# Row maxima beside the projections, all taken as key differences: 208 double steps a layer, 20 pairs a block in attention

## The chip, the cores and the metric

The kernel runs on one core of a Trainium2 chip. The core has five engines with their own instruction streams: TensorE (PE in the profile; its weight loads have the row PEld), VectorE (DVE), ScalarE (ACT), GpSimd (POOL), and SyncE (SP), which here issues nearly all DMAs. Each engine executes its instructions in order and waits on semaphores. Matmuls write to PSUM, which has eight banks of 128 x 512 fp32. The metric is the device time of one execution in microseconds (us).

## The reference

Two layers with the same weights, each an attention and a feed-forward part with a residual, on 2048 tokens of width 640 with 32 heads of 20:

```python
def _A_ref(x, wqkv, wo):
    qkv = (x @ wqkv).reshape(B, S, 3, H, Dh).transpose(2, 0, 3, 1, 4)
    q, k, v = qkv[0], qkv[1], qkv[2]
    scores = jnp.einsum("bhqd,bhkd->bhqk", q, k) * (Dh ** -0.5)
    p = _softmax(scores, axis=-1)
    o = jnp.einsum("bhqk,bhkd->bhqd", p, v)
    return o.transpose(0, 2, 1, 3).reshape(B, S, D) @ wo

def _B_ref(x, w1, b1, w2, b2):
    h = x @ w1 + b1
    r = jnp.where(h > 0, h, 0)
    return (r * r) @ w2 + b2

x = A_x
x = x + _A_ref(_layernorm(x), A_wqkv, A_wo)
x = x + _B_ref(_layernorm(x), B_w1, B_b1, B_w2, B_b2)
x = x + _A_ref(_layernorm(x), A_wqkv, A_wo)
x = x + _B_ref(_layernorm(x), B_w1, B_b1, B_w2, B_b2)
```

The sizes are B = 1, S = 2048, D = 640, H = 32, Dh = 20, F = 1536, all in fp32.

## The kernel before

Each layer runs in four stages: projections (`qkv`), attention, output projection, feed-forward. Factors of the projections are split into a high and a low part of a rounded format, so a product is three matmuls (high by high, and the two mixed ones).

**Maxima ahead of scores.** The softmax subtracts the exact row maximum. It has to be known before the scores are made, since it enters the score matmul as two more rows of the query tile (L753 multiplies 62 rows, 60 of the three split products and 2 of the maximum). So the product of queries and keys is made twice. First it is made with queries on the partitions (`by_queries`, L659), and VectorE reduces each 128 x 512 result along the keys. Later it is made with keys on the partitions for the exponentials (`score`, L753). Heads are handled in groups of four. A *block* t is one group and 512 queries: 8 groups by 4 query tiles are 32 blocks. For one block and one tile c of 512 keys there are eight *pairs*: a pair is two matmuls (L659) of 128 queries for two heads. They lie in rows 0 to 59 and 64 to 123 and run side by side on the two row halves of TensorE. Counted in these pairs, each layer has 32 blocks x 4 key tiles x 8 = 1024 pairs.

**Single and double steps.** A single step is a pair, with a `tensor_reduce` on VectorE for each of its two results. A double step finds the maximum over two key tiles k1 and k2 from max(q·k1, q·k2) = relu(q·(k1 − k2)) + q·k2. `step_two` makes a pair with the key difference `kd`, and ScalarE writes its relu to SBUF (L692). `both_two` makes a pair with the other key tile, and VectorE adds and reduces in one custom operation for each result, followed by a read of its accumulator (L699). So a double step takes two pairs on TensorE, but only two operations on VectorE for two key tiles. The difference "d" is of key tiles 0 and 1, "e" of 2 and 3. Differences are made in `proj_end` while keys leave the projection. They are stored to the DRAM tensor `d_kd` and loaded again by `load_kd`, rearranged by heads with six DMAs. Keys (`load_k`) and queries (`load_q`) make the same trip through `d_qk`, with six DMAs each.

**The projections.** There are 40 units of query and key columns (128 columns by 512 tokens, 15 matmuls), the list `UNITS`: first the columns 0 to 3 of token block 0, then the same of block 1, 2 and 3, then the other six columns for all blocks. So units 0 to 3 belong to token block 0, units 4 to 7 to block 1, 8 to 11 to block 2, and 12 to 15 to block 3. The column at place 0 is the first key tile of 128 rows, at place 2 the second, at place 4 the third. Then come 16 V units of 30 shorter matmuls. From unit 4 on each matmul is cut into an upper and a lower half of 64 rows, which run side by side (L356 and L368). The lower halves trail by 19 matmuls (`LAG`), so that after the last V unit 18 lower halves are left alone. After each matmul `between(cost)` pays the cost (1, or 0.65 in a V unit) into a pace; when it is used up, `some()` issues one pair, and the pace rises by `PLAIN_PACE` for a single or `DOUBLE_PACE` for a double. `STEPS` says after which unit which tiles are loaded and which maxima may begin. The same loop advances the normalising of the next token block (`front`): statistics and scaling on VectorE, transposes on TensorE. In layer 1 the rows of token block 2 are transposed in unit 6 and those of block 3 in unit 9; in layer 2 those of block 3 in unit 6.

**Attention.** What is left of the pairs is taken there, before the block that needs it. The order of TensorE is a string of letters, `ORDER_OF_BLOCK`, 16 key tiles of 128 long and repeated. "a" and "b" are a score matmul on one row half with a 128 x 512 exponential behind it (L763). "S" is both at once with one 128 x 1024 exponential. "m" and "n" are a maximum matmul on one row half (L659, reduced at L670). "V" is the value product of one key tile (L768): four heads on four column quarters, which the trace shows as eight matmuls. A *gap* is what lies between two V. `todo` lists what the projections left.

**Queues.** A DMA on SP waits for the data it stores or for the store whose data it loads, and everything behind it in the queue waits too.

## Time and profile before

| what | us |
|---|---|
| median of three runs (3578.84 to 3579.93) | 3579.07 |
| the profiled execution | 3581.79 |
| its span in the trace | 3580.0 |
| TensorE busy | 3555.0 |
| ScalarE busy | 2694.4 |
| VectorE busy | 2643.6 |
| GpSimd busy | 835.1 |

By the value matmuls and the first projections, layer 1 has its projections until about 344.6 us and its attention until about 1388. Output projection and feed-forward follow until about 1801, the projections of layer 2 until 2116, and its second attention until about 3162. In a timeline a row gives the start, the length, the engine, the line of the code, the operation and the tiles, how many were merged, and in brackets the idle time before it with what ended it. In a table by stretches a row gives the stretch, its length, for each engine the busy time and the count of instructions, then the granted clock of TensorE, the busy share of the DMA engines and GB/s. Where the table was asked for one line of the code, only that line's instructions are counted.

### The profile page before, as it was taken

The numbers are of one execution on the slowest core, as the hardware profiler recorded it, in microseconds if no ns is written. First come the engines' busy times: TensorE is split into PE (matmuls) and PEld (weight loads), VectorE is DVE, ScalarE is ACT, GpSimd is POOL, SyncE is SP. The second block draws the span as 40 slices with busy tenths as digits, with TensorE's granted clock in tenths as the row PEclk, the third lists the DMA queues.
The fourth block names the chain that finished last, engine by engine and source line by source line (L and its number), as shares of the span: only waits on it lengthen the run. The fifth ranks groups of instructions, "written<-read, shape, count | busy, mean of one in ns | idle before, by whom it ended". The sixth has DMA issues, their size and how long they took to land.

```text
span 3580.0 us, 70922 instructions
## 1 busy us (share of the span) xinstructions
PE 3555.0 (99%) x25544; PEld 2148.8 (60%) x25544; DVE 2643.6 (74%) x5072; ACT 2694.4 (75%) x4742; POOL 835.1 (23%) x945
## 2 busy tenths in 40 slices
PE   9999999999999999999999999999999999999999
PEld 7898333333333336988989973333333333378998
DVE  8999888888888881445579988888888888625443
ACT  3888999999999995122248889999999999932221
POOL 5440334312121211112143201212121212101110
PEclk9999999999999999999999999999999999999999
DMA  7666454422222136622356652222222121365221
GB/s 242 225 229 195 134 173 144 148 74 73 56 55 57 54 106 203 250 74 74 103 192 226 196 172 67 79 75 61 69 82 57 45 57 51 112 237 206 75 81 37
DMA packets 282799, 433.85 MB, mean 121 GB/s; under 512 B 71188, under 2 KB 130324, under 8 KB 282448
## 3 DMA queue, kind: packets, MB, share of 16 engines
q1 hardware_dynamic: 281920, 427.61, 38.3%
q8 instruction: 203, 3.33, 0.4%
q10 hardware_dynamic: 528, 1.70, 0.2%
q14 instruction: 148, 1.21, 0.1%
HBM read 284.48 MB, written 144.68 MB: 120 GB/s over the span
## 4 chain that ended last, share of the span: by engine, by line
PE 94%; DMA 2%; DVE 2%; ACT 1%; issue 0%; SPq 0%; POOL 0%; ACTq 0%; DVEq 0%; POOLq 0%
PE banks L768 28%; PE banks L336 21%; PE banks L753 18%; PE banks L659 17%; PE banks L368 5%; PE banks L356 5%; PE banks L351 1%; PE banks L466 0%; DMA d_qk<-ev 0%; SPq L76 0%; ACT e L763 0%; DMA few<-d_s 0%; DVE r L1283 0%; DVE h L257 0%; ACT r L1282 0%
## 5 line engine op out<-in xcount | busy, mean ns | idle before, releaser
L763 ACT ACTIVATE e<-banks 128x512 f32<-128x512 f32 (+1 forms) x3460 | 2040.1, 688 | 49.1 <-PE banks L753 10.7
L670 DVE TENSOR_REDUCE mx<-banks 128x1 f32<-128x512 f32 x2560 | 1620.0, 684 | 323.1 <-PE banks L659 276.3
L768 PE MATMUL banks<-e,vg 128*32 128x512 f32 x8192 | 1096.4, 605 | 6.1 <-ACT e L763 5.4
L659 PE MATMUL banks<-k,q 60*128 60x512 f32 x3392 | 1073.1, 411 | 5.0 <-DVE mx L684 3.1
L753 PE MATMUL banks<-q,k 62*128 62x512 f32 x4096 | 1043.3, 440 | 0.0
L753 PEld LDWEIGHTS banks<-q,k 62*128 62x128 f32 x4096 | 513.6, 184 | 741.6 <-ACT e L763 468.0
L659 PEld LDWEIGHTS banks<-k,q 60*128 60x128 f32 x3392 | 573.8, 185 | 205.9 <-ACT e L763 65.6
L699 DVE CUSTOM_DVE_ANT_0 rl<-banks,rl 128x512 f32<-128x512 f32 x704 | 456.7, 688 | 32.6 <-PE banks L659 9.3
L692 ACT ACTIVATE rl<-banks 128x512 f32<-128x512 f32 x704 | 382.2, 601 | 55.5 <-PE banks L659 44.6
L768 PEld LDWEIGHTS banks<-e,vg 128*32 128x32 f32 x8192 | 163.8, 108 | 362.7 <-issue 263.1
L336 PE MATMUL banks<-w,h 128*128 128x320 f32 x2304 | 348.9, 310 | 2.7 <-DVE h L257 2.5
L1282 ACT ACTIVATE r<-banks,b_t 128x512 f32<-128x512 f32 x96 | 66.1, 689 | 375.9 <-PE banks L336 203.0
L336 PEld LDWEIGHTS banks<-w,h 128*128 128x128 f32 x2304 | 339.2, 188 | 11.4 <-DVE h L257 6.4
L336 PE MATMUL banks<-xnT,w 128*128 128x512 f32 x1440 | 329.7, 389 | 0.0
L356 PE MATMUL banks<-xnT,wqk 64*128 64x512 f32 x1080 | 327.9, 395 | 0.0
L368 PE MATMUL banks<-xnT,wqk 64*128 64x512 f32 x1080 | 327.8, 393 | 0.0
L336 PEld LDWEIGHTS banks<-xnT,w 128*128 128x128 f32 x1440 | 269.6, 188 | 55.3
L812 POOL TENSOR_TENSOR few<-few,minus_t 128x16 f32<-128x16 f32 x62 | 179.8, 2900 | 228.4 <-DMA few<-d_s 228.3
L368 PEld LDWEIGHTS banks<-xnT,wqk 64*128 64x128 f32 x1080 | 201.9, 187 | 9.4
L659 PE MATMUL banks<-kd,q 60*128 60x512 f32 x704 | 205.2, 397 | 1.8 <-ACT rl L692 1.0
L356 PEld LDWEIGHTS banks<-xnT,wqk 64*128 64x128 f32 x1080 | 199.7, 187 | 11.1 <-issue 1.9
L268 POOL CAST mr<-nt 128x32 fp32r<-128x32 f32 x64 | 13.4, 210 | 817.8 <-DVE nt L725 817.8
(90 smaller groups left out, 2766.3 us busy)
## 6 DMA issues: line engine op xcount, KB each, us to landing
q<-d_qk SPq DMA_DIRECT2D x888, 80.0 KB
d_qk<-ev SPq DMA_DIRECT2D x80, 512.0 KB
k<-d_qk SPq DMA_DIRECT2D x456, 80.0 KB
x<-d_x SPq DMA_DIRECT2D x96, 320.0 KB
d_o<-ot SPq DMA_DIRECT2D x248, 80.0 KB
ot<-d_o SPq DMA_DIRECT2D x38, 512.0 KB
d_v<-v SPq DMA_DIRECT2D x32, 512.0 KB
vg<-d_v SPq DMA_DIRECT2D x32, 512.0 KB
```

The costliest lines, as they stand in the source:

```text
L336: nc.tensor.matmul(dst, a, b, start=(n == 0), stop=(n == last))
L356: top = nc.tensor.matmul(dst, a[:64], b[:64], start=start, stop=last)
L368: low = nc.tensor.matmul(dst, a, b, start=False, stop=last, skip_group_check=True)
L659: nc.tensor.matmul(dst, q_t[t][b : b + 60, p, sub * P : (sub + 1) * P], k_t[t // NQB, c][b : b + 60, p, :], start=True, stop=True,)
L670: nc.vector.tensor_reduce(maxima(t)[:, 2 * p + par, sub, c : c + 1], dst, axis=AX.X, op=ALU.max)
L692: nc.scalar.activation(r, dst, AF.Relu)
L699: nc.vector.tensor_tensor_reduce(out=r[par], in0=dst, in1=r[par], scale=1.0, scalar=LEAST, op0=ALU.add, op1=ALU.max, accum_out=maxima(t)[: ...
L753: nc.tensor.matmul(dst, k_t[t // NQB, kt // 4][b : b + 62, p, (kt % 4) * P : (kt % 4 + 1) * P], q_t[t][b : b + 62, p, :], start=True, stop ...
L763: nc.scalar.activation(dst, src, AF.Exp, scale=SCALE)
L768: nc.tensor.matmul(acc[32 * h : 32 * h + 32, :], v_t[t // NQB, kt // 8][:, kt % 8, 32 * h : 32 * h + 32], es[p][:, par, :], start=(kt == 0 ...
L812: nc.gpsimd.tensor_tensor(few, few, minus_t, op=ALU.pow)
L1282: nc.scalar.activation(r, dst, AF.Relu, bias=b1_t[:, f : f + 1])
```

## The change

- In attention `ORDER_OF_BLOCK` has 20 "m" and "n" pairs in 16 key tiles where it had 21 (42 letters become 40), and 9 "S" where it had 10. Once no maxima are left, another string, `LAST_ORDER`, with "S" and "V" alone, takes over.
- In the projections the four groups of single steps (32 pairs) are gone. `DOUBLE` has 26 groups of eight double steps where it had 22: 208 steps, or 416 pairs, where 32 single and 176 double steps made 384. Attention is left with 608 pairs in place of 640 a layer.
- `DOUBLE_PACE` is 1.90 where it was 1.97. Maxima begin after unit 8 (double) where singles began after unit 4 and doubles after unit 12.
- Key differences are made for three key row tiles instead of two (`jj < 3`; `d_kd` grows to match). For token block 1 and the first two of them the three steps run on VectorE instead of GpSimd, and the store is issued 6 matmuls after the unit's end where it was 16.

What this does to the order of instructions is shown at three places. In TensorE's queue in the first attention, at the start of the same block of both programs (L753 becomes L756, L659 becomes L662, L768 becomes L771; a value product is two rows of two here). Before:

```order
L753 MATMUL banks<-q_7511,k_1184 128x512 x2
L659 MATMUL banks<-k_4452,q_7568 128x512 x2
L753 MATMUL banks<-q_7511,k_1184 128x512 x2
L659 MATMUL banks<-k_4452,q_7568 128x512
L768 MATMUL banks<-e_5398,vg_7877 32x512 x2
L768 MATMUL banks<-e_5397,vg_7877 32x512 x2
L659 MATMUL banks<-k_4452,q_7568 128x512
L753 MATMUL banks<-q_7511,k_1184 128x512 x2
L659 MATMUL banks<-k_4452,q_7568 128x512 x2
L753 MATMUL banks<-q_7511,k_1184 128x512 x2
```

and of the change:

```order
L756 MATMUL banks<-q_7690,k_1116 128x512 x3
L662 MATMUL banks<-k_4581,q_7856 128x512 x2
L756 MATMUL banks<-q_7690,k_1116 128x512
L771 MATMUL banks<-e_5599,vg_8052 32x512 x2
L771 MATMUL banks<-e_5598,vg_8052 32x512 x2
L756 MATMUL banks<-q_7690,k_1116 128x512 x3
L662 MATMUL banks<-k_4581,q_7856 128x512 x2
L756 MATMUL banks<-q_7690,k_1116 128x512
```

The gaps here hold four scores and two maximum matmuls where they held four and three. Over the 16 gaps of a block ten held seven matmuls and six held six; now it is eight and eight.

SP's queue in the first layer, from the store of unit 3's result on (`ev`; `d_qk<-ev_575` and `d_qk<-ev_529` are unit 4's). Before:

```order
L76 DMA d_qk<-ev_420 128x2x512
L76 DMA x_469<-in_A_x_dram 128x640
L76 DMA x_471<-in_A_x_dram 128x640
L76 DMA x_473<-in_A_x_dram 128x640
L76 DMA x_475<-in_A_x_dram 128x640
L76 DMA k_477<-d_qk 20x2x512 x6
L76 DMA q_484<-d_qk 20x2x512 x6
L76 DMA d_wqk<-wqk_283 128x1024
L76 DMA d_qk<-ev_575 128x2x512
L76 DMA d_kd<-kd_580 128x2x512
L76 DMA k_721<-d_qk 20x2x512 x6
L76 DMA q_728<-d_qk 20x2x512 x6
```

and of the change:

```order
L76 DMA d_qk<-ev_406 128x2x512
L76 DMA x_455<-in_A_x_dram 128x640
L76 DMA x_457<-in_A_x_dram 128x640
L76 DMA x_459<-in_A_x_dram 128x640
L76 DMA x_461<-in_A_x_dram 128x640
L76 DMA d_wqk<-wqk_283 128x1024
L76 DMA d_qk<-ev_529 128x2x512
L76 DMA d_kd<-kd_534 128x2x512
L76 DMA kd_581<-d_kd 20x2x512 x6
L76 DMA k_588<-d_qk 20x2x512 x6
L76 DMA q_595<-d_qk 20x2x512 x6
```

The key and query loads for single steps are gone from ahead of the first key difference. Its store is followed at once by its own load, and the first keys and queries stand behind that load. In layer 2 the same pieces stand in the same order, with nothing between the stores of units 0 to 3 and unit 4's store. TensorE's first maximum matmul, which needs `kd` and `q` of these, stands three matmul steps into unit 9.

TensorE's queue at the end of the projections, from the last of the 18 lower halves (L368) on. Before:

```order
L368 MATMUL banks<-wv_3059,xnT_866 128x320
L368 MATMUL banks<-wv_3162,xnT_866 128x320
L368 MATMUL banks<-wv_3059,xnT_866 128x320
L753 MATMUL banks<-q_2225,k_4443 128x512 x7
L659 MATMUL banks<-k_4846,q_4855 128x512 x2
```

and of the change:

```order
L368 MATMUL banks<-wv_3193,xnT_808 128x320
L662 MATMUL banks<-kd_5013,q_4803 128x512 x2
L662 MATMUL banks<-k_5020,q_4803 128x512 x2
L662 MATMUL banks<-kd_5013,q_4803 128x512 x2
L662 MATMUL banks<-k_5020,q_4803 128x512 x2
L662 MATMUL banks<-kd_5013,q_4803 128x512 x2
L662 MATMUL banks<-k_5020,q_4803 128x512 x4
L756 MATMUL banks<-q_2171,k_4581 128x512 x6
```

Seven pairs now stand between the last projection matmul and the first scores. Beside the units, the program of the change has eight pairs in nearly every unit from 10 to 39 and ten or eleven in a V unit; before, it had two to five in units 5 to 14, seven or eight after that, and nine or ten in a V unit.

The diff, cut to its core:

```diff
@@ proj_end
-        if which and pos < FIRST:
-            if tb % 2 == 0 and jj == 0:
+        if which and jj < 3:
+            if tb % 2 == 0 and jj != 1:
                 keys["of"] = slot([P, 2, QB], F32, "kf")
-            kf = keys["of"][:, jj, :]
+            kf = keys["of"][:, jj % 2, :]
             r = xtile("r")[:, :QB] if tb % 2 else kf
-            split_on_pool(ev[:, 0, :], ev[:, 1, :], dst, r, nc.scalar.copy)
+            split_on_pool(
+                ev[:, 0, :], ev[:, 1, :], dst, r, nc.scalar.copy if pos < FIRST else None
+            )
             if tb % 2:
                 kd = slot([P, 2, QB], F32R, "kd")
-                nc.gpsimd.tensor_sub(kf, r, kf)
-                pool_hi(kd[:, 0, :], kf)
-                pool_lo(kd[:, 1, :], kf, kd[:, 0, :].bitcast(F32))
+                eng = nc.vector if pos < FIRST and tb == 1 else nc.gpsimd
+                eng.tensor_sub(kf, r, kf)
+                eng.tensor_copy(kd[:, 0, :], kf)
+                eng.tensor_sub(kd[:, 1, :], kf, kd[:, 0, :].bitcast(F32))
@@ the tables
     DOUBLE = [
-        [],
-        [(0, 1, "d"), (1, 1, "d"), (2, 0, "d"), (2, 1, "d")],
+        [(0, 0, "d"), (0, 1, "d")],
+        [(1, 0, "d"), (1, 1, "d"), (2, 0, "d"), (2, 1, "d")],
         [(0, 2, "d"), (1, 2, "d"), (2, 2, "d")],
...
+        [(3, 0, "d"), (3, 0, "e")],
     ]
-    PLAIN_PACE = 4.2
-    DOUBLE_PACE = 1.97
+    DOUBLE_PACE = 1.90
     STEPS = {
-        2: [("tiles", (0, 0, 0))],
-        4: [("plain", (0, 0, 0)), ("tiles", (1, 0, 0))],
-        5: [("plain", (1, 0, 0))],
-        7: [("tiles", (0, 0, 1))],
-        9: [("plain", (0, 0, 1)), ("tiles", (1, 0, 1))],
-        10: [("tiles", (0, 1, "d"))],
-        11: [("plain", (1, 0, 1))],
+        6: [("tiles", (0, 0, "d"))],
+        8: [("double", 0)],
+        9: [("tiles", (1, 0, "d"))],
         12: [("double", 1)],
         15: [("double", 2)],
         19: [("double", 3)],
+        26: [("double", 4)],
     }
@@ qkv
-                later(store, 10 if n < FIRST else 16)
+                later(store, 10 if n < FIRST else 6 if tb == 1 and pos in (0, 2) else 16)
@@ attention
     ORDER_OF_BLOCK = (
-        "bbannaVbamnabmVnabmnabVSnanbmVnambabmVSbmnaVSnabmVSnSmVbmamnSVbmanbanVan"
-        "abmbmVbambannVbmabanmVSmbanVSnabmVSnSmVm"
+        "SnabmVSanmbVSanmbVSSmnVnabbanmVnabanmbVbabmnnaVnaabmbmVbmmbanaVnambmbaVb"
+        "amnmbaVnanbabmVSmnabVSmnabVSnabmVSanmbV"
     )
+    LAST_ORDER = "SSSVSSVSSVSV"
...
-            for o in ORDER_OF_BLOCK:
+            for o in LAST_ORDER if min(sm_n) == len(todo) else ORDER_OF_BLOCK:
                 op(o)
```

Left out are the function `one` for single steps, which goes, and the loads of the first keys and queries of attention, which follow the new list of what is left.

More of the change, by code (lines that the diff above doesn't have):

```diff
@@ L882, in qkv @@
     def qkv(first, x_src, rest):
-        pending, groups, work = [], [], []
+        pending = []
         double, twos, begun = [], [], []
@@ L940, in end_group @@
             t = g * NQB + qb
-            rest = [w[0] for w in work[:1] + twos[:1]] + [w[0][0] for w in begun[:1]] + groups + double
+            rest = [w[0] for w in twos[:1]] + [w[0][0] for w in begun[:1]] + double
             if t == 0:
@@ L967, in following @@
             return queue.pop(0)
-        def one():
-            w = following(groups, work)
-            if w:
-                (g, qb, c), p, sub = w
-                smax_two(g * NQB + qb, p, sub, c)
-                done.add((g * NQB + qb, p, sub, c))
-                if (p, sub) == PAIRS[-1]:
-                    end_group(w[0])
         def some():
@@ L992, in some @@
                 return DOUBLE_PACE
-            if groups or work:
-                one()
-                return PLAIN_PACE
             w = following(double, twos)
```

19 lines of the change are left out of this document (9 added, 10 removed).

## The prediction, made before the result was known

> **What bounds the kernel now.** I read the page first, then attention as TensorE issues it, then the projections by stretches, then the start of each.
>
> ```profile
> PE 3555.0 (99%) x25544; PEld 2148.8 (60%) x25544; DVE 2643.6 (74%) x5072; ACT 2694.4 (75%) x4742; POOL 835.1 (23%) x945
> 2643.00:2970.10 327.10, 170.30 (x1280) 25.01 (x1272) 1.00 0.22 60
> 2643.00:2970.10 327.10, 137.22 (x420) 72.00 (x420) 1.00 0.22 60
> 2643.00:2970.10 327.10, 318.91 (x540) 1.00 0.22 60
> 1358.49:1388.32 29.83, 27.43 (x185) 7.55 (x185) 0.00 (x0) 28.71 (x52) 6.08 (x4) 1.00 0.56 171
> ```
>
> TensorE is busy nearly always, but its matmuls overlap, so that alone settles nothing. Rows two to four are one stretch of the second attention, by line: L768 (values), L659 (maxima), L763 (exponentials on ScalarE). 1280 value matmuls are 160 key tiles, ten blocks of 16: 32.71 us a block with 42 maximum matmuls (21 pairs). ScalarE is busy 318.91 of 327.10 us, 97.5%, so it looks like the bound. The last row denies it: the last 16 key tiles of the first attention, with all their exponentials and no maxima, took 29.83 us. ScalarE can therefore do a block in 29.83; the other 2.9 come with the maxima. How, a piece of the timeline shows:
>
> ```profile
> 871.49 0.50 PE L659 MATMUL banks<-k,q 60*128 60x512 f32 x1
> 871.49 0.73 PE L753 MATMUL banks<-q,k 62*128 62x512 f32 x2
> 871.83 0.62 PE L659 MATMUL banks<-k,q 60*128 60x512 f32 x2
> 872.07 0.62 PE L753 MATMUL banks<-q,k 62*128 62x512 f32 x2
> 872.61 1.07 PE L768 MATMUL banks<-e,vg 128*32 128x512 f32 x8
> ...
> 876.85 1.06 PE L768 MATMUL banks<-e,vg 128*32 128x512 f32 x8
> ...
> 879.74 0.73 PE L753 MATMUL banks<-q,k 62*128 62x512 f32 x3
> 880.08 0.39 PE L659 MATMUL banks<-k,q 60*128 60x512 f32 x1
> 880.31 0.39 PE L753 MATMUL banks<-q,k 62*128 62x512 f32 x1
> 880.31 0.40 PE L659 MATMUL banks<-k,q 60*128 60x512 f32 x1
> ...
> 882.54 1.06 PE L768 MATMUL banks<-e,vg 128*32 128x512 f32 x8
> ```
>
> The first four rows fill one gap between value groups: 4 scores and 3 maxima. From 872.61 to 876.85 lie two more such gaps, 2.12 us each. From 876.85 to 882.54 lie three with 4 scores and 2 maxima, as in the second group of rows: 1.90 each. The two kinds run on the two row halves side by side, so 3+4 matmuls take four turns and 3+3 take three; a turn is 0.225 us. Half a turn is wasted in each gap of seven. TensorE's order is the bound of attention.
>
> In the projections:
>
> ```profile
> 1848.27:1865.42 17.15, 16.13 (x61) 11.15 (x60) 1.00 0.76 222
> 1848.27:1865.42 17.15, 5.54 (x28) 2.62 (x28) 1.00 0.76 222
> 1941.00:1994.18 53.18, 47.21 (x151) 28.05 (x150) 1.00 0.74 234
> 1941.00:1994.18 53.18, 39.69 (x155) 23.50 (x154) 1.00 0.74 234
> 2012.82:2113.50 100.68, 100.68 (x1197) 100.66 (x1196) 97.26 (x298) 88.97 (x179) 7.86 (x17) 1.00 0.59 184
> ```
>
> Rows one and three count L356 (15 to a unit), two and four L659. Four units with 14 pairs take 17.15 us, ten units with 77 pairs 53.18. Two equations: a unit costs 3.43 us and a pair 0.245, so TensorE's issue sets the time here too. The last row is fifteen V units: 6.71 us each, and VectorE 97.26 of 100.68 busy on 149 double operations, 0.653 us each.
>
> **The change, part by part.** *Attention gets 608 pairs instead of 640 and 20 a block instead of 21.* The new string has 8 gaps of seven and 8 of six, the old 10 and 6. Two gaps a block lose a turn: 2 x 0.225 = 0.45 us. 608/20 = 30.4 blocks: -13.7 us a layer. In the last block only wide exponentials are issued, which by the 28.71 us of ScalarE there can save little; with one pair fewer in the block before I take -0.6 (bounds -1 to +2). So -14.3 a layer, **-28.6**. ScalarE's work hides behind it: it would have to slow from 29.83 to over 32.26 a block to undo the gain.
>
> *The 32 pairs go beside the projections.* 32 x 0.245 = 7.8 us a layer, **+15.7**. VectorE has as many operations as before there (416: 64 single and 352 double, now all double). With the shorter pace a V unit gets 19.5/1.90 = 10.26 pairs, 6.71 + 0.33 x 0.245 = 6.79 us; VectorE needs 10.26 x 0.653 = 6.70. It still fits, barely; if it were the bound at 100.68/149 = 0.676 a pair, it would add 0.14 x 16 = 2.2 us a layer. I take nothing, and keep that.
>
> *Seven pairs now stand after the last projection matmul.*
>
> ```profile
> 2113.54 2.80 PE L368 MATMUL banks<-wv,xnT 64*128 64x320 f32 x18
> 2119.26 1.07 PE L768 MATMUL banks<-e,vg 128*32 128x512 f32 x8
> 2019.22 0.69 DVE L699 CUSTOM_DVE_ANT_0 rl<-banks,rl 128x512 f32<-128x512 f32 x1
> 2019.84 0.69 DVE L699 CUSTOM_DVE_ANT_0 rl<-banks,rl 128x512 f32<-128x512 f32 x1
> ```
>
> Before, scores followed the 18 matmuls at once. Now three difference pairs and four key pairs do; the four need eight VectorE operations, 0.62 us apart back to back: 5.0 us. With five banks the last pair leaves some 3.7 us after the first, of which 7 x 0.245 = 1.7 is counted: +2.0 a layer, **+4.0**. Bounds: 0, if the first value group would wait for exponentials anyway, to 5.0 - 1.7 = 3.3.
>
> *No maxima run in units 5 to 8, so VectorE is free for the normalising of token blocks 2 and 3.*
>
> ```profile
> 34.06:72.74 38.68, 11.64 (x32) 5.44 (x32) 0.91 0.78 255
> 1824.30:1848.27 23.97, 7.58 (x32) 3.90 (x32) 1.00 0.62 196
> 61.64 0.50 PE L659 MATMUL banks<-k,q 60*128 60x512 f32 x1 [1.30 <-DVE mx L684]
> ```
>
> Both stretches are units 5 to 9 with 16 pairs. In layer 2, 23.97 = 5 x 3.43 + 16 x 0.245 + 2.9 for one set of transposes. Layer 1 has two sets: 26.9, and took 38.68. The 11.8 us over are waits like the third row's, where a maximum stands behind statistics on VectorE, and a granted clock that is 0.91 in the mean: a loss of 0.09 x 38.68 = 3.5 us, as 7 us at half clock would give. With the maxima gone I take all of it: **-11.8**. Bounds: -6, if half of it waits for DMAs and stays, to -12.
>
> *But the doubles now begin at unit 9, and need a key difference that has made the trip through DRAM.* What stands there now:
>
> ```profile
> 1829.88 0.58 ACT L263 COPY r<-banks 128x512 f32<-128x512 f32 x1 [8.45 <-PE banks L659]
> 1834.48 1.27 POOL L271 TENSOR_TENSOR kd<-kf,kd 128x512 fp32r<-128x512 f32 x1
> 1835.79 0.38 SPq L76 DMA_DIRECT2D d_kd<-kd  x1
> 1838.95 2.89 SPq L76 DMA_DIRECT2D q<-d_qk  x6
> 1863.41 7.17 DMA d_qk<-ev
> 1870.60 6.15 DMA kd<-d_kd
> 1876.76 3.53 DMA kd<-d_kd
> L1283 DVE TENSOR_TENSOR r<-r 128x512 f32<-128x512 f32 x96 | 78.3, 815 | 136.7 <-ACT r L1282 131.6 <-DMA y<-d_t 5.0
> ```
>
> In layer 2 GpSimd's three steps end 1835.75, and the store follows. After the change ScalarE's copy comes 1 us sooner (four pairs fewer in unit 5) and VectorE does the steps in about 2.1 us (two subtractions by the 815 ns row, a cast below that): store at 1831.6. Landed some 3 us later (bounds: 2, and 7.17 by the store in the chain), SP then issues six loads each of kd, k and q, all queued behind the wait: 3 x 2.5 = 7.5 us (the q row has 2.89 for its six) to 1842.1, and the last lands 3.5 later (the row 1876.76; 6.15 at worst): 1845.4. TensorE's first double comes three matmul steps into unit 9, at 1824.30 + 4 x 3.43 + 2.9 (transposes) + 0.7 = 1841.6. It waits 3.7 us, everything in TensorE's queue behind it, projections too. In layer 1, by the same steps, 4.0: **+7.7**. Bounds: 1 and 10.5 a layer. A wait of that size may bring the half clock again: 7 us at half speed, as in layer 1 now, costs 3.5 us; at less than even odds 1.5 a layer, **+3.0**.
>
> The Trainium skill speaks against the change here: "TensorE: Matmul & The Clock Gate", Part 1, says that a window of about 3.4 us without work halves the clock until a busy window has passed. By it a wait of 3.7 us costs one half-speed window more, 1.7 us (an estimate from that page), and a wait below 3 costs nothing; the sum would move by under 4 us. The low clock in the trace followed several short waits, not one window of idleness, so the odds stay.
>
> *The rest I cost at nothing.* GpSimd still makes four difference tiles a layer, about 3.3 us each: two move to VectorE, and two of the third key tile come, used more than ten units later; it is busy 23%. Two stores and two groups of loads more a layer are needed as late. VectorE's two tiles, 4.2 us, fall where its maxima were; without that cover they would hold the statistics queued behind them for as long.
>
> *An old wait goes:* the first difference was loaded late before as well.
>
> ```profile
> 1870.06:1882.52 12.46, 9.46 (x32) 5.47 (x32) 1.00 0.62 191
> ```
>
> Units 15 and 16 with 16 pairs: 12.46 against 2 x 3.43 + 16 x 0.245 = 10.8. These 1.7 us a layer go: **-3.4** (bounds 0 and -5).
>
> Sum: -28.6 + 15.7 + 4.0 - 11.8 + 7.7 + 3.0 - 3.4 = **-13.4 us**. The profiled execution has a span of 3580.0 and a time of 3581.79, 2.7 above the median; I take the sum from the median: 3579.07 - 13.4 = 3565.7, so 3566.
>
> **Rivals.** *ScalarE holds attention.* Eight gaps of six now stand in a row across a block's border, and each must fit a wide and two narrow exponentials into 1.90 us. If ScalarE's 97.5% is the true bound, blocks stay at 32.7 and the moved maxima are pure cost: 3579 + 15.2 = 3594, slower. It decides from a gain under 15.2/60.8 = 0.25 us a block. For it: the 97.5%. Against: 29.83 us without maxima, and gaps that follow the turns within 0.02 us.
>
> *The trip through DRAM is as slow as in the chain* (7.17, then 6.15): 10.5 us of waiting a layer, 13.3 more in all: 3579, no change. For it: those rows, and DMA at 0.6 to 0.8 of its share. Against: they stand where weight loads share the queues; units 6 to 8 have none of these in layer 2.
>
> *The wait hides*: DMAs land in 2 to 3 us, no half clock, the seven last pairs cost only their own time: 7.7 becomes 2.2, 3.0 and 4.0 go, 12.5 less than the forecast: 3553. For it: kd and q loads queue on quiet DMAs in layer 2. Against: SP issues eighteen of them one by one.
>
> **Numbers.** Forecast 0.70, the slow trip 0.15, hidden waits 0.10, ScalarE 0.05. Below 0.2% (7.2 us) a measurement cannot tell a change, so faster means under 3571.9. Of the forecast 0.64 lies there and 0.06 within; the hidden case is faster; the slow trip is 0.01 faster, 0.12 same, 0.02 slower; ScalarE slower. Faster 0.75, same 0.18, slower 0.07. The range takes in the hidden waits and most of the slow trip: 3553 to 3577.
>
> **What would show it.** Blocks of 32.2 to 32.3 us in both attentions with 40 maximum matmuls; gaps still 1.90 and 2.12. Projection units with eight pairs at 5.4 us, V units at 6.8. A wait of TensorE on DMA at the first double, 2 to 6 us, and perhaps a half clock behind it. Units 5 to 8 of layer 1 without waits. Some 9 us from the last V unit to the first value group instead of 5.8. I am wrong if blocks stay above 32.5, if VectorE stalls the V units, or if the first double waits over 8 us.

## The result: slower, and the profile after

The changed kernel takes 3602.51 us, the median of four runs (3601.8 to 3603.55), beside 3579.5 us (3578.84 to 3581.25) of the kernel before in the same runs: a ratio of 1.0058, with a 95% interval of 1.0046 to 1.007. It is slower by 23 us, where the prediction had it faster by 13. The profiled execution has a span of 3601.0 us, 21.0 more than the 3580.0 of before.

Attention did much of what was predicted. First the three lines of it, in a stretch of ten blocks of the second attention (start and end, length, busy time and count on TensorE, or on ScalarE alone in the third row, then granted clock, DMA share and GB/s); the lines are L771 (values), L662 (maxima) and L766 (exponentials):

```profile
2671.69:2995.07 323.38, 170.46 (x1281) 25.46 (x1282) 1.00 0.22 60
2671.69:2995.07 323.38, 118.20 (x401) 62.22 (x400) 1.00 0.22 60
2671.69:2995.07 323.38, 317.17 (x551) 1.00 0.22 60
```

A block takes 32.34 us with 40 maximum matmuls, where it took 32.71 with 42. Next both attentions from the first value product to the last (columns: TensorE, its weight loads, VectorE, ScalarE, GpSimd), after and then before:

```profile
365.26:1395.56 1030.30, 1027.81 (x7344) 383.31 (x7343) 801.37 (x1308) 1009.08 (x1734) 274.15 (x290) 1.00 0.35 100
2152.14:3183.04 1030.90, 1028.73 (x7343) 384.02 (x7342) 801.13 (x1308) 1008.18 (x1733) 202.83 (x186) 1.00 0.26 72
```

```profile
344.55:1387.25 1042.70, 1039.61 (x7408) 395.73 (x7407) 837.90 (x1372) 1018.01 (x1726) 273.34 (x290) 1.00 0.34 100
2119.26:3161.66 1042.40, 1039.36 (x7410) 396.69 (x7409) 837.84 (x1372) 1017.87 (x1726) 202.03 (x186) 1.00 0.26 73
```

That is 12.4 us less in layer 1 and 11.5 less in layer 2. So the loss lies in the projections. Here are their stretches after: units 5 to 8, unit 9, units 10 to 17 and the end (from the end of the last V unit to the first value product) of layer 1, then unit 9, units 10 to 17 and the end of layer 2:

```profile
34.57:51.09 16.52, 16.52 (x137) 13.31 (x137) 11.40 (x22) 9.05 (x16) 13.12 (x15) 1.00 0.53 185
51.09:72.81 21.72, 11.85 (x66) 7.85 (x64) 8.65 (x21) 9.97 (x19) 10.39 (x13) 0.76 0.64 211
72.81:122.17 49.36, 46.48 (x372) 37.66 (x370) 41.90 (x131) 43.52 (x84) 21.50 (x20) 1.00 0.58 186
...
353.05:365.26 12.21, 10.25 (x51) 6.33 (x48) 7.66 (x25) 8.28 (x16) 0.00 (x0) 0.90 0.62 232
...
1849.12:1862.50 13.38, 8.24 (x46) 6.46 (x43) 4.08 (x12) 5.13 (x10) 1.70 (x2) 0.74 0.72 242
1862.50:1909.88 47.38, 46.00 (x371) 38.01 (x369) 41.77 (x131) 42.12 (x80) 16.62 (x14) 1.00 0.71 237
...
2140.15:2152.14 11.99, 10.94 (x52) 6.65 (x48) 7.67 (x25) 8.95 (x17) 0.00 (x0) 0.82 0.68 235
```

and the same of before, units 10 to 17 of layer 1, then units 10 to 17 and the end of layer 2 (the end of layer 1 took 5.73):

```profile
72.74:112.11 39.37, 38.67 (x326) 34.80 (x324) 34.58 (x81) 24.68 (x45) 22.04 (x20) 1.00 0.69 224
...
1848.27:1887.95 39.68, 38.66 (x326) 32.04 (x324) 34.57 (x81) 23.05 (x43) 17.39 (x15) 1.00 0.71 218
...
2113.52:2119.26 5.74, 5.74 (x35) 4.21 (x31) 2.83 (x10) 2.87 (x7) 0.00 (x0) 1.00 0.66 267
```

The reader is to see three places where TensorE's busy time falls short of the stretch or its clock below 1.00: unit 9, units 10 to 17, and the end. The table sets both layers beside the prediction's terms, sorted into the same stretches. For that the 15.7 us of moved pairs are spread by where the pairs went: 9 fewer a layer in units 5 to 9, 22 more in units 10 to 17, 12 more after those, 7 more at the end, 0.245 us each.

| stretch, both layers, us | predicted | measured | missed by |
|---|---|---|---|
| units 5 to 9 (-11.8 freed, +7.7 wait, +3.0 clock, -4.4 pairs) | -5.5 | -0.4 + 5.9 = +5.5 | 11.0 |
| units 10 to 17 (+10.8 pairs, -3.4 old wait) | +7.4 | +10.0 + 7.7 = +17.7 | 10.3 |
| units 18 to 39 and V units (+5.9 pairs) | +5.9 | +8.9 | 3.0 |
| the end (+3.4 pairs, +4.0) | +7.4 | +6.5 + 6.2 = +12.7 | 5.3 |
| attention | -28.6 | -12.4 - 11.5 = -23.9 | 4.7 |
| sum | -13.4 | +20.9 | 34.3 |

The 49.36 us of units 10 to 17 in layer 1 hold some 1.3 us of this one execution: in four of the runs below that leave these units as they are, the stretch takes 48.0.

**Unit 9.** TensorE in layer 1 and in layer 2, at its first maximum matmuls:

```profile
59.90 0.76 PE L662 MATMUL banks<-kd,q 60*128 60x512 f32 x1 [8.19 <-DMA q<-d_qk]
61.71 0.76 PE L662 MATMUL banks<-kd,q 60*128 60x512 f32 x1 [1.04 <-DMA q<-d_qk]
...
1853.79 0.47 PE L662 MATMUL banks<-kd,q 60*128 60x512 f32 x1 [4.05 <-DMA q<-d_qk]
1855.35 0.76 PE L662 MATMUL banks<-kd,q 60*128 60x512 f32 x1 [1.09 <-DMA q<-d_qk]
```

It stands idle for 9.2 and 5.1 us, for the queries, the last of eighteen loads. The clock is halved, not just lower: taken in steps of 1 us, it reads 0.50 in every step from 56 to 65 us. So the mean clocks of 0.76 and 0.74 in the rows above mean that half clock held for (1 - 0.76) x 21.72 / 0.5 = 10.4 us and 7.0 us, part of it while TensorE still waited. Now the chain that these loads end, from the queues of ScalarE (the copy of unit 4's keys in each layer), of VectorE (the three steps of the first difference in layer 1, a step of the second one, then the first difference in layer 2) and of SyncE in layer 2:

```profile
42.85 0.58 ACT L263 COPY r<-banks 128x512 f32<-128x512 f32 x1
...
1837.10 0.59 ACT L263 COPY r<-banks 128x512 f32<-128x512 f32 x1 [7.37 <-PE banks L368]
```

```profile
43.47 1.61 DVE L406 TENSOR_TENSOR kf<-r,kf 128x512 f32<-128x512 f32 x1 [4.81 <-ACT r L263]
45.11 1.40 DVE L407 CAST kd<-kf 128x512 fp32r<-128x512 f32 x1
46.55 1.67 DVE L408 TENSOR_TENSOR kd<-kf,kd 128x512 fp32r<-128x512 f32 x1
...
53.35 0.43 DVE L407 CAST kd<-kf 128x512 fp32r<-128x512 f32 x1
...
1837.71 0.69 DVE L406 TENSOR_TENSOR kf<-r,kf 128x512 f32<-128x512 f32 x1 [5.70 <-ACT r L263]
1838.44 1.54 DVE L407 CAST kd<-kf 128x512 fp32r<-128x512 f32 x1
1840.02 1.67 DVE L408 TENSOR_TENSOR kd<-kf,kd 128x512 fp32r<-128x512 f32 x1
```

```profile
1841.72 0.36 SPq L76 DMA_DIRECT2D d_kd<-kd  x1
1844.70 2.19 SPq L76 DMA_DIRECT2D kd<-d_kd  x6
1846.99 2.18 SPq L76 DMA_DIRECT2D k<-d_qk  x6
1849.21 2.84 SPq L76 DMA_DIRECT2D q<-d_qk  x6
```

In layer 2 each step of the prediction can be laid beside this. The copy came when predicted, and so did the landing of the store (1844.70 - 1841.72 = 2.98) and the eighteen issues (7.35). The last load took 3.3 us to land, not 6 to 7, so the rival of the slow trip did not come. But the three steps on VectorE took 3.95 us (1837.71 to the store), not 2.1. In layer 1 they took 4.75, and the copy itself came 4.9 us after unit 6 began (37.97) instead of 1.1 (1835.99), since there the transposes and six ScalarE instructions of the token block stood ahead of it. The second difference of layer 1, beside which GpSimd had little but operations on 128x1, shows VectorE's own price: 0.68, 0.43 and 0.69. In layer 2 the first step took 0.69 while GpSimd was idle; GpSimd then began its subtractions at 1838.41, and the next two took 1.54 and 1.67. So the slowdown follows GpSimd's work; that it is the port both use is not shown by these rows alone. The Trainium skill, "SBUF — State Buffer", section "SBUF: two separate sides", has such a rule: VectorE operations with two SBUF inputs or in a two-port mode and GpSimd's share one port pair, which one instruction holds to its end. By it a step may wait for one GpSimd instruction; the extra 0.9 to 1.1 us a step fits, since GpSimd's own subtractions take 1.3 us there.

**Units 10 to 17.** ScalarE in unit 11 of layer 2, and TensorE behind it:

```profile
1869.26 1.09 ACT L695 ACTIVATE rl<-banks 128x512 f32<-128x512 f32 x2 [0.31 <-PE banks L662]
1870.39 0.59 ACT L263 COPY r<-banks 128x512 f32<-128x512 f32 x1
1871.01 0.62 ACT L264 CAST ev<-r 128x512 fp32r<-128x512 f32 x1
1871.53 2.05 ACT L695 ACTIVATE rl<-banks 128x512 f32<-128x512 f32 x4
```

```profile
1872.18 0.49 PE L662 MATMUL banks<-kd,q 60*128 60x512 f32 x1 [0.36 <-ACT rl L695]
```

A double step needs ScalarE for its relus. The result of each of units 8 to 15 gives ScalarE a copy and a rounding as well, 1.2 us, during which the relus pile up (four in a row, 2.05) and the banks of the difference pairs stay full. Eight relus at 2.05/4 = 0.51 and these 1.2 make 5.3 us in a unit that should last 5.4. Singles, which stood in units 10 to 14 before, need no ScalarE: it ran 3 relus there in layer 1, and 24 in units 15 to 17.

**The end.** TensorE in layer 2 from the last lower halves to the first value product:

```profile
2140.62 2.51 PE L368 MATMUL banks<-wv,xnT 64*128 64x320 f32 x16
...
2144.58 0.49 PE L662 MATMUL banks<-kd,q 60*128 60x512 f32 x1 [0.54 <-ACT rl L695]
...
2147.31 3.32 PE L756 MATMUL banks<-q,k 62*128 62x512 f32 x7
...
2152.14 1.08 PE L771 MATMUL banks<-e,vg 128*32 128x512 f32 x4
```

The seven pairs last from 2142.83 to 2147.3. What they wait for is mostly ScalarE: its relus are late (the row with 0.54), because the copy of the last V result stands ahead of them and waits for the lower halves. Of the waits of their weight loads 1.6 us are for ScalarE and 0.4 for VectorE, which then holds up the scores. These run at half clock: seven take 3.32 us, 0.47 apart. The first blocks of attention still feel it, with 34.2 and 35.0 us where they took 33.1 before.

### The profile page after: what moved, and what is told of

Its sections match the earlier page's. It is cut to its first block, busy times and chain, and to the rows that moved or that the text cites. A ratio compares the mean times of both kernels' runs of the same rounds, so it can differ in the third digit from the quotient of the medians.

```text
span 3601.0 us, 71125 instructions
## 1 busy us (share of the span) xinstructions
PE 3561.0 (99%) x25544; PEld 2137.5 (59%) x25544; DVE 2582.9 (72%) x5086; ACT 2743.8 (76%) x4888; POOL 839.5 (23%) x945
## 4 chain that ended last, share of the span: by engine, by line
PE 92%; DMA 2%; ACT 2%; DVE 1%; issue 1%; SPq 1%; POOL 1%; POOLq 0%; ACTq 0%; DVEq 0%
PE banks L771 27%; PE banks L336 21%; PE banks L756 17%; PE banks L662 16%; PE banks L368 6%; PE banks L356 4%; ACT e L766 1%; SPq L76 1%; PE banks L351 1%; PE banks L469 0%; DMA x<-d_x 0%; DMA k<-d_qk 0%; DVE h L257 0%; DVE r L1271 0%; ACT r L1270 0%
## 5 line engine op out<-in xcount | busy, mean ns | idle before, releaser
L766 ACT ACTIVATE e<-banks 128x512 f32<-128x512 f32 (+1 forms) x3478 | 2024.7, 684 | 46.9 <-PE banks L756 25.5
L673 DVE TENSOR_REDUCE mx<-banks 128x1 f32<-128x512 f32 x2432 | 1547.4, 685 | 371.4 <-PE banks L662 291.8
L771 PE MATMUL banks<-e,vg 128*32 128x512 f32 x8192 | 1095.7, 606 | 4.1 <-ACT e L766 3.0
L756 PE MATMUL banks<-q,k 62*128 62x512 f32 x4096 | 1041.4, 442 | 1.5 <-DVE mx L702 0.7
L662 PE MATMUL banks<-k,q 60*128 60x512 f32 x3264 | 947.4, 410 | 1.6 <-DVE mx L673 0.7
L756 PEld LDWEIGHTS banks<-q,k 62*128 62x128 f32 x4096 | 511.9, 185 | 649.1 <-ACT e L766 396.7
L662 PEld LDWEIGHTS banks<-k,q 60*128 60x128 f32 x3264 | 508.9, 185 | 299.6 <-ACT e L766 201.6
L702 DVE CUSTOM_DVE_ANT_0 rl<-banks,rl 128x512 f32<-128x512 f32 x832 | 536.3, 688 | 62.2 <-PE banks L662 28.8
L695 ACT ACTIVATE rl<-banks 128x512 f32<-128x512 f32 x832 | 449.9, 601 | 79.6 <-PE banks L662 72.0
L771 PEld LDWEIGHTS banks<-e,vg 128*32 128x32 f32 x8192 | 163.8, 108 | 363.8 <-ACT e L766 195.0
L356 PE MATMUL banks<-xnT,wqk 64*128 64x512 f32 x1080 | 336.5, 398 | 0.0
L368 PE MATMUL banks<-xnT,wqk 64*128 64x512 f32 x1080 | 335.5, 395 | 0.0
L662 PE MATMUL banks<-kd,q 60*128 60x512 f32 x832 | 237.0, 406 | 20.0 <-DMA q<-d_qk 14.4
L368 PEld LDWEIGHTS banks<-xnT,wqk 64*128 64x128 f32 x1080 | 203.1, 189 | 12.7
```

Source lines behind the costliest of these rows:

```text
L356: top = nc.tensor.matmul(dst, a[:64], b[:64], start=start, stop=last)
L368: low = nc.tensor.matmul(dst, a, b, start=False, stop=last, skip_group_check=True)
L662: nc.tensor.matmul(dst, q_t[t][b : b + 60, p, sub * P : (sub + 1) * P], k_t[t // NQB, c][b : b + 60, p, :], start=True, stop=True,)
L673: nc.vector.tensor_reduce(maxima(t)[:, 2 * p + par, sub, c : c + 1], dst, axis=AX.X, op=ALU.max)
L695: nc.scalar.activation(r, dst, AF.Relu)
L702: nc.vector.tensor_tensor_reduce(out=r[par], in0=dst, in1=r[par], scale=1.0, scalar=LEAST, op0=ALU.add, op1=ALU.max, accum_out=maxima(t)[: ...
```

## The experiments

All kernels are the changed one with an edit, except the one that says otherwise. Spans are of the profiled execution; the changed kernel has 3601.0. The first seven are one execution each, and four executions of the changed kernel spread over 1.8 us, so a difference in span of that size is not told from chance.

**First keys and queries loaded early.**

```diff
     STEPS = {
+        2: [("tiles", (0, 0, 0))],
         6: [("tiles", (0, 0, "d"))],
```

> The loads of the first keys and queries (twelve DMAs) are issued after unit 2, as in the kernel before; only the six loads of the key difference stay behind its store. Theory (the wait at unit 9 is mostly SP issuing eighteen loads one after the other behind the difference's store): the first double finds its tiles 4 to 5 us sooner. Layer 2: idle time of TensorE there from 5.1 us (4.05 and 1.09) to about 1, no half clock behind it, unit 9 from 13.4 to 6 to 7 us. Layer 1: idle from 9.2 us to about 4.5, unit 9 from 21.7 to 12 to 16 us, with the half clock shorter or gone. In all 11 to 17 us less than the changed kernel. Rival (the trip of the difference itself, its steps, its store and its own six loads, sets the wait): both waits stay within 1 us and so does the time. Units 10 to 17 stay at 5.8 to 6.1 in either case.

The span is 3584.8, 16.2 less. Unit 9 takes 14.94 us in layer 1 and 6.16 in layer 2 (21.72 and 13.38). TensorE there in layer 1:

```profile
53.98 0.47 PE L662 MATMUL banks<-kd,q 60*128 60x512 f32 x1 [2.62 <-DMA kd<-d_kd]
55.42 0.47 PE L662 MATMUL banks<-kd,q 60*128 60x512 f32 x1 [0.97 <-DMA kd<-d_kd]
```

It now waits for the difference itself, 3.6 us in place of 9.2; in layer 2 no load is waited for. Twelve loads in SP's queue were most of the price. The rival falls.

**Rounding of units 8 to 15 off ScalarE.** (And the same in the other branch of `proj_end`.)

```diff
-                ev[:, 0, :], ev[:, 1, :], dst, r, nc.scalar.copy if pos < FIRST else None
+                ev[:, 0, :], ev[:, 1, :], dst, r, nc.scalar.copy if pos < FIRST and tb < 2 else None
```

> The rounding of the results of units 8 to 15 (a copy to the high part, 0.62 us each) goes from ScalarE to GpSimd, as it is for all later units. Theory (in units 10 to 17 ScalarE is late with the relus, so the banks of the difference pairs come free late and TensorE waits): units 10 to 17 fall from 5.8 to 6.1 us to 5.4 to 5.6, 3 to 5 us a layer, 6 to 10 us in all. Rival one (these units wait for late DMA loads of tiles, as the prediction said of units 15 and 16): no change, and with GpSimd's steps later perhaps 1 us slower. Rival two (VectorE, 16 doubles of 0.62 us in 5.4 us with its other work, is the limit): no change. The wait at unit 9 and the end of the projections stay.

Span 3589.9, 11.1 less. Units 10 to 17 of the two layers:

```profile
71.95:115.81 43.86, 43.86 (x370) 41.62 (x368) 41.44 (x131) 39.25 (x76) 25.38 (x28) 1.00 0.62 200
1855.96:1899.45 43.49, 43.49 (x371) 42.02 (x369) 41.39 (x131) 37.81 (x73) 21.63 (x22) 1.00 0.79 256
```

5.5 us a unit, TensorE busy to the last hundredth, with VectorE's work unchanged (131 instructions): 9.4 us of the 11.1 are these units, or some 8 beside the 48.0 that layer 1 takes in other runs. Late loads and VectorE, which are as they were, are ruled out as the cause of these 8.

**The same in the kernel before,** as a test of the step that the prediction called an old wait.

```diff
-            split_on_pool(ev[:, 0, :], ev[:, 1, :], dst, r, nc.scalar.copy)
+            split_on_pool(ev[:, 0, :], ev[:, 1, :], dst, r, nc.scalar.copy if tb < 2 else None)
```

> The kernel before the change, with the rounding of the results of units 8 to 15 on GpSimd instead of ScalarE, nothing else. It tells what the slow units 15 and 16 of that kernel (12.46 us in layer 2 where 10.8 would do) wait for. Theory now (ScalarE, where those copies stand between the relus of the first doubles): units 15 and 16 fall to 10.8 to 11.2 us in both layers, 3 to 4 us in all. Rival, the step of the prediction (the first difference is loaded late): they stay at 12.4 and so does the time.

Units 15 and 16, which took 11.94 us in layer 1 and 12.46 in layer 2, took 10.88 here in layer 1:

```profile
96.01:106.89 10.88, 10.88 (x94) 10.45 (x92) 10.29 (x31) 9.63 (x20) 7.23 (x8) 1.00 0.58 168
```

and 11.06 in layer 2. The wait was ScalarE's, not that of a late load. The time hardly moved (3581.02 beside 3581.81), because units 5 to 8 got longer in that kernel, by 1.4 us in layer 1 and 0.6 in layer 2. So of the 3 to 4 us expected 2.5 showed in the two units and 0.8 in the whole.

**A pace of 1.86,** which leaves no pair behind the last projection matmul.

```diff
-    DOUBLE_PACE = 1.90
+    DOUBLE_PACE = 1.86
```

> The pace is 1.86 where it was 1.90, so that no pair is left behind the last projection matmul: scores follow at once. Theory (the seven pairs at the end leave TensorE waiting for VectorE's banks, and the idle time brings half clock on the scores): from the end of the last V unit to the first value group 6 to 7 us instead of 12.2 and 12.0, no half clock there, and the first block back at 33 us; 10 to 12 us in all. Rival one (the half clock there comes from the value group's own wait for exponentials and stays): 3.5 to 4 us less a layer at the end, 7 in all. Rival two (VectorE is the bound of the V units at 1.90 already): V units go up by 0.1 to 0.15 us each, 2 us a layer, which takes back half of it.

Span 3591.2, 9.8 less. The end of layer 2:

```profile
2138.85:2144.53 5.68, 5.53 (x35) 4.03 (x31) 2.01 (x7) 2.92 (x7) 0.00 (x0) 1.00 0.85 316
```

The end takes 5.68 in place of 11.99 with no half clock, and the first block 32.4 in place of 35.0. The seven pairs now run beside the units, and units 18 to 39 take 3.3 us more in layer 1 and 1.9 in layer 2, the V units 0.9 and 0.8. The whole loss of clock at the end went with the pairs that had been left there.

**Differences on GpSimd again.**

```diff
-                eng = nc.vector if pos < FIRST and tb == 1 else nc.gpsimd
+                eng = nc.gpsimd
```

> The two key differences of token block 1 are made on GpSimd again, as in the kernel before; all else as changed. Theory (the three steps took 3.95 and 4.7 us on VectorE, since GpSimd runs beside it, where the prediction had 2.1): GpSimd's three steps take some 3.8 us but stand behind its other work, so the store comes 1 to 3 us later and the wait at unit 9 grows by as much, 2 to 5 us in all with its half clock; it also shows whether VectorE's steps run at 0.4 to 0.7 us when GpSimd does not run beside them. Rival (the move to VectorE is what delays the statistics of the next token block, so that the transposes in unit 9 come late): the time falls.

Span 3602.3, 1.3 more. Measured from the start of unit 5, the store in layer 2 is issued 1.3 us later, and unit 9 takes 14.29 us (13.38); in layer 1 unit 9 takes 21.28 (21.72), while units 5 to 8 take 1.1 us more as TensorE waits for GpSimd's parts of the token block. By units 5 to 9 the move to VectorE was worth 0.7 and 0.9 us; the span alone would not tell it. GpSimd's own steps took 1.30, 0.61 and 1.29, less in all than VectorE's 3.95 and 4.75 beside it, so what the move gained is the time behind GpSimd's other work.

**Dummy matmuls in the wait of unit 9.**

```diff
+                if not state.get("warm"):
+                    state["warm"] = 1
+                    warm(50 if first else 26)
                 begun.append((w, step_two(g * NQB + qb, p, sub, x)))
```

> Ahead of the first difference pair of each layer TensorE gets dummy matmuls on data that is there (50 in layer 1, 26 in layer 2, some 0.14 us each by the transposes of the same size, so about 7 and 3.6 us), inside the time in which it waits anyway. Theory (the half clock behind the wait of unit 9 comes from that idle time, and costs about 3 us a layer): the granted clock stays 1.0 from 50 us on and from 1854 us on, unit 9 falls from 21.7 to 18 to 19 us in layer 1 and from 13.4 to about 10 in layer 2, 6 us in all. Rival one (the half clock comes from something else, such as the start of the doubles on all engines at once): clock and time stay. Rival two (the dummies last longer than the wait): the time rises by what is over, 1 to 3 us.

Unit 9 of both layers:

```profile
50.69:72.96 22.27, 20.85 (x167) 17.36 (x164) 8.63 (x21) 9.64 (x19) 10.36 (x13) 1.00 0.63 196
...
1848.91:1861.99 13.08, 11.87 (x98) 10.24 (x96) 4.10 (x12) 4.91 (x10) 1.69 (x2) 1.00 0.67 229
```

The clock stays at 1.00: idle time made it fall. But unit 9 hardly changed, and the span fell by only 2.3 us. Each dummy was two matmuls in the trace, and the 100 and 52 of them took 11.43 and 6.07 us, not 7 and 3.6. In layer 1 the first difference pair follows them at once, so rival two may hold there, and its 22.27 us do not tell the price of the clock. In layer 2 the last load landed 7.5 us into unit 9 where it had landed 6.0 into it, because some loads took longer. From that landing to the unit's end it took 5.5 us instead of 7.4. So the half clock cost up to 1.9 us there, near the 1.5 a layer that the prediction allowed, and not the 3 expected here: TensorE also waits for ScalarE in this stretch. (With the old string, below, the same projections took 6.4 from the landing to the end at the same length of half clock, which makes it 0.9; the price is 1 to 2 us.)

**The old string with the new projections.**

```diff
     ORDER_OF_BLOCK = (
-        "SnabmVSanmbVSanmbVSSmnVnabbanmVnabanmbVbabmnnaVnaabmbmVbmmbanaVnambmbaVb"
-        "amnmbaVnanbabmVSmnabVSmnabVSnabmVSanmbV"
+        "bbannaVbamnabmVnabmnabVSnanbmVnambabmVSbmnaVSnabmVSnSmVbmamnSVbmanbanVan"
+        "abmbmVbambannVbmabanmVSmbanVSnabmVSnSmVm"
     )
```

> Attention goes by the old string again (21 pairs and ten gaps of seven in a block), with the 608 pairs and the last string of the change. Theory (TensorE's turns set a block, 32.3 us with the new string and 32.7 with the old): 608/21 = 28.95 blocks of 32.71 and 3.05 without maxima of 28.1 us make 1032.7, where the new string by the same count makes 30.4 x 32.35 + 1.6 x 28.1 = 1028.4: 4 us a layer, 8 to 9 us in all slower than the changed kernel, with blocks of 32.7. Rival (the block is set by ScalarE, and fell because there are fewer pairs in attention): blocks stay at 32.3 and, since more of them have no maxima, a layer's attention gets 6 us shorter. The projections do not change.

Span 3610.8, 9.8 more; attention takes 1037.23 us in both layers, 6.9 and 6.3 more. (The projections, where nothing is edited, were 3.3 us shorter in this execution.) Maxima in ten blocks of the second layer:

```profile
2681.51:3008.91 327.40, 137.50 (x421) 72.03 (x420) 1.00 0.22 60
```

A block has 32.74 us again, as the theory of turns said; the rival, ScalarE, would have left it at 32.3 and shortened attention. Of the 12.4 us that attention gained in layer 1, 5.5 come from fewer pairs and the last string (1042.7 to 1037.2) and 6.9 from the new string. That is more than the 4 us a layer that the theory counted; what the rest is was not looked for.

**The three repairs together:** the diffs of the early loads, of the rounding and of the pace.

> The changed kernel with the early first loads, the rounding of units 8 to 15 on GpSimd, and the pace 1.86. If the three costs are separate: 3602.5 - 15.9 - 10.8 - 9.5 = 3566, 0.4% faster than before. If ScalarE and the late loads hid each other in part (units 10 to 17 of layer 1 shared their waits), 3568 to 3571. If VectorE becomes the bound when the units run at 5.4 us with a shorter pace, units 10 to 17 go up to 5.5 to 5.6 and the time to 3570 to 3575.

3573.29 us (3571.46 to 3574.6) beside 3581.81 of before: 0.9977, interval 0.9967 to 0.9986. It is faster than the kernel before by 8.5 us; three separate costs would have made 3566. Unit 9 and units 10 to 17 of layer 1:

```profile
50.54:67.22 16.68, 11.15 (x69) 7.88 (x66) 9.84 (x24) 10.88 (x21) 11.27 (x14) 0.90 0.63 205
67.22:111.52 44.30, 44.30 (x374) 41.42 (x371) 41.27 (x131) 39.25 (x76) 24.86 (x27) 1.00 0.64 201
```

That is 5.54 us a unit, and with the time it is the third case of the expectation; that VectorE is the bound there is not shown. Unit 9 is 1.7 us longer than with the early loads alone, with one pair more in it, and in units 33 to 37, which take up to 6.2 us, relus are late again (layer 1 splits raw weights on ScalarE there). The span is 30.8 below the changed kernel's, where the three edits alone had 16.2 + 11.1 + 9.8 = 37.1.

**Layer 1 one unit later,** on top of the three.

```diff
-            for what, x in STEPS.get(n, ()):
+    PACE = {True: 1.82, False: 1.86}
...
+            steps = STEPS.get(n, [])
+            if first and n in (8, 9):
+                steps = [] if n == 8 else STEPS[8] + STEPS[9]
+            for what, x in steps:
```

> The kernel with the three edits, and in layer 1 the doubles start one unit later (unit 10) at a pace of 1.82, so that they still end with the last projection matmul. Theory (what is left of the wait in unit 9 of layer 1, 2.96 and 0.91 us of idle time and a stretch of half clock, is the difference's own trip, which ends some 4 us after TensorE asks for it): with the transposes now ahead of the first double there is no wait; unit 9 takes 6.3 us with no pair where it took 16.7 with eight, the eight pairs cost 2 us elsewhere: 8 us less, 3565 beside a kernel before of 3581.8. Rival (VectorE is the bound at the shorter pace, 8.24 pairs a unit of 0.62 us and more): units 10 to 39 of layer 1 go from 5.5 to 5.7 us, V units from 6.9 to 7.1, which takes all of it back.

3571.57 us (3571.31 to 3572.09) beside 3580.55: 0.9972 (0.9962 to 0.9983), which cannot be told from the kernel without this edit. Unit 9 has no pair now and still takes 12.79 us, 3.9 less. Units 10 to 39 took 2.6 us more and the V units 1.1, where 2 were expected for eight more pairs; so a part of the rival's price shows, and the two together took the gain back. TensorE in unit 9, at the transposes:

```profile
55.89 0.33 PE L469 MATMUL banks<-ident,x 128*128 128x128 f32 x1 [2.93 <-DVE x L252]
57.36 2.71 PE L469 MATMUL banks<-ident,x 128*128 128x128 f32 x10 [1.14 <-DVE x L252]
```

A second wait lay beneath the first: the rows of token block 3 are late, since their statistics stand behind the differences in VectorE's queue, which itself waits for ScalarE's copy (the row at 43.47 above has 4.81 us of idle time in front of it).

**The differences of layer 1 on GpSimd,** on top of that.

```diff
-                eng = nc.vector if pos < FIRST and tb == 1 else nc.gpsimd
+                eng = nc.vector if pos < FIRST and tb == 1 and not keys["first"] else nc.gpsimd
```

> The kernel of the run before, with the key differences of token block 1 in layer 1 on GpSimd. There unit 9 of layer 1 still took 12.79 us instead of 6.3: TensorE's transposes wait for the rows of token block 3 (0.16, 2.93 and 1.14 us of idle time and half clock behind), whose statistics stand in VectorE's queue behind the key differences. Theory: without these VectorE starts the statistics when the rows have landed, the transposes do not wait, the difference itself is 1 to 2 us later and still in time for unit 10: unit 9 falls to 6.3 to 7.5 us, units 5 to 8 lose 1.1 us to GpSimd as in the earlier run with its differences there; 4 to 5 us less in all, 3567 beside 3580.6. Rival (the rows or the difference land late by themselves, since SP now issues the first keys and queries ahead of the rows): unit 9 stays above 10 us and the time does not move.

It gained nothing: 3578.31 us (3576.73 to 3580.49) beside 3581.93, 0.999 (0.9981 to 0.9999), by the ratios slower than the run before it, though the two intervals just touch. TensorE in layer 1, in unit 11:

```profile
80.53 0.76 PE L662 MATMUL banks<-kd,q 60*128 60x512 f32 x1 [4.54 <-DMA q<-d_qk]
```

The statistics were early, but their last step, a power on GpSimd, now stood behind the differences there, so TensorE still waited for the rows (the longest wait is 1.51 us) and unit 9 stayed at 12.85. The second difference left GpSimd later too, SP held the loads behind its store, and TensorE waited 4.5 us for queries in unit 11. The expectation had looked at one queue where the work stood in three.

## Why the prediction was wrong

Two steps failed most. The wait for the first difference came out at 14.4 us where the sum had 7.7 (within the bounds of 1 to 10.5 a layer, but in layer 1 above the 8 us that the prediction called its sign of being wrong). And ScalarE's work in units 10 to 17 had no term in the sum at all.

*Attention: right in mechanism.* Blocks fell to 32.34 us (32.26 forecast), ScalarE did not hold them, and the old string brought them back. Of the 4.7 us missed, 4.4 are the first blocks' half clock, which belongs to the end: with the pace of 1.86 they take 32.40 and 32.47 us in place of 34.21 and 35.01. Both attentions of the kernel with the three repairs:

```profile
352.20:1380.78 1028.58, 1026.06 (x7343) 383.69 (x7342) 801.98 (x1308) 1009.97 (x1735) 273.82 (x290) 1.00 0.35 101
2124.04:3152.22 1028.18, 1026.02 (x7344) 383.52 (x7343) 801.66 (x1308) 1010.05 (x1735) 202.55 (x186) 1.00 0.26 74
```

There attention gains 28.3 us where 28.6 were forecast.

*The wait for the first difference (+7.7): the step that failed was its length.* Two costs in it were wrong. The 2.1 us for VectorE's steps came from a row of subtractions at 815 ns and took no account of GpSimd beside them: 3.95 and 4.75. And layer 1 was worked out "by the same steps" as layer 2, at 4.0, though its copy stands behind the transposes: 9.2 of idle time. The queueing of eighteen loads was rightly seen, and it is the larger part: with twelve of them moved 14.0 us of the two units 9 went. The rival of a slow trip named 10.5 us a layer, near what layer 1 showed, but by a landing that did not come.

*The freed waits of layer 1 (-11.8): units 5 to 8 gave what was said* (16.52 us, no wait), *but what unit 9 was to gain was taken by the new wait,* and the last runs show another beneath: the sentence that VectorE's differences would hold the statistics "without that cover" came true behind ScalarE's late copy.

*The half clock (+3.0): about right in size,* 1 to 2 us by the runs in layer 2, with some luck (3.0 was a price of 3.5 a layer taken at less than even odds), but only half of the places were named. The scores behind the seven last pairs ran at half clock as well.

*The old wait (-3.4): wrong cause.* It was put down to a late load; ScalarE's copies in units 8 to 15 made it. Read rightly, it was a warning: with doubles in place of singles the two slow units became eight. The prediction checked ScalarE in attention and let it pass in the projections; this omission cost most of the 10.3 us, and some 8 of them went when the copies moved.

*The seven pairs (+4.0): a wait, as said, but not that one alone, and size off.* The pairs waited for ScalarE's relus more than for VectorE. The end grew by 12.7 us instead of 7.4, mostly since its scores ran at half clock: by the mean clocks for 2.4 and 4.3 us, which costs half of that, 3.4. The pace of 1.86 took all of it away.

*The pairs beside units 18 to 39 and V units: short by 3 us.* The cause is open. VectorE, busy for 106.4 of the 111.1 us of the V units, is a candidate, the bound that the prediction had priced at 2.2 us a layer and set at nothing; but TensorE shows next to no wait there, and no run tried it.

What stays open is unit 9 of layer 1: no run here made it short, and the right order of its work on three engines was not found.

## What to carry to other kernels

When work of one kind takes the place of another kind, list what every engine does for it in the very units where it now runs: here five of eight units got an engine in their path that the old work there hardly used. A first transfer that gates an in-order queue should have only its own loads behind its store; whatever is ready earlier goes ahead of it. And when a wait is taken out, look for the one beneath it before counting the gain: of 37 us that three repairs gave one by one, 31 were left together, and two further edits gave nothing.

## What was not expected of the hardware

The clock fell to half not only behind one long wait but at the end of the projections, where the longest idle time of TensorE ahead of the fall is 0.54 us in layer 2 and 0.73 in layer 1, with matmuls between. In layer 2 it was then low for (1 - 0.82) x 11.99 / 0.5 = 4.3 us before the first value product and (1 - 0.91) x 35.01 / 0.5 = 6.3 in the block behind it, 10.6 in all (in steps of half a us, it reads 0.50 from 2148 to 2158). The block's row is:

```profile
2152.14:2187.15 35.01, 34.98 (x234) 12.82 (x233) 26.07 (x45) 30.45 (x54) 0.93 (x4) 0.91 0.40 105
```

The stretches in unit 9 were 10.4 and 7.0. The Trainium skill, "TensorE: Matmul & The Clock Gate", Part 1, says that the clock is set window by window, 3.4 us each, and falls after an idle one. The lengths agree with two and three such windows; the fall at the end, with no window idle, does not follow from that sentence.

In the run with dummy matmuls some loads took longer, in both layers. In layer 2 a load of keys, issued before the dummies began, took 5.38 us to land where one of the six took 3.69 without them. SyncE's later loads of queries waited for that landing, but then took 3.15 us (3.32 without), with dummies still running. So it is not all loads beside them, and why was not tried.
